# One second-weight load cut into 112, 8 and 8 rows with a small load between the last two

## The chip, the core and the metric

The kernel runs on one core of a Trainium2 chip. The metric is the device time of one execution in microseconds (us), and the median of several executions is what counts. The core has five engines with instruction streams of their own: TensorE (PE; its weight loads are listed as PEld), VectorE (DVE), ScalarE (ACT), GpSimd (POOL) and SyncE (SP). Sixteen DMA engines move data between the chip's main memory (HBM) and the core's on-chip memory of 128 partitions. An engine that issues a transfer goes on at once; a semaphore tells when the data has landed.

## The reference

Two layers follow each other. The first is attention with a sliding window, for 8 batches and 8 heads of 576 positions and 64 dimensions. Heads 0 to 3 see the last 32 positions, heads 4 to 7 every fourth of the last 128. The second is a soft mixture of experts over all 8 x 576 = 4608 tokens of 512 features:

```python
x = attn_out.transpose(0, 2, 1, 3).reshape(B * S, H * D)
logits = x @ phi                                  # 4608 x 32 slots
d = softmax of logits over the tokens             # per slot
slot_input = (d.T @ x).reshape(8, 4, 512)         # 8 experts, 4 slots each
for e in range(8):
    slot_out[e] = np.maximum(slot_input[e] @ w1[e], 0) @ w2[e]   # 512 -> 1024 -> 512
c = softmax of logits over the slots              # per token
return c @ slot_out                               # 4608 x 512, float32
```

All inputs are float32 in HBM. No expert can run before the last token's attention is done, because a slot's input sums over all tokens. w1 and w2 are 16 MB each.

## The kernel before, in words

**Work and order.** Attention runs in eight units (two batches by four heads each). For each unit POOL loads q, k and v into one of three staging buffers (`stg`), with the cast from float32 to bfloat16 done in the transfer; TensorE transposes them (L546, L551), computes scores (L589), transposes v (L614), multiplies by v (L643) and transposes the result (L671); logits and slot sums follow after every second unit (L698, L729, L746). Then come the experts: the slot sums are brought into shape (L798), the first layer (L817), a transposition (L837), the second layer (L864), row sums (L880), and at last the output product (L923, L925), its scaling on ACT and DVE (L937, L938) and the stores by SP (L946).

**The planner.** The program is a list of operations with a planned cost, a due time and dependencies. `schedule` (from L170) plays it through on a clock of its own and so fixes the order in which each engine gets its instructions; `emit` then writes waits on semaphores. POOL's and SP's operations keep the order in which they are listed. The planner has one clock, `dma_free`, for all transfers:

```python
o.dma = nbytes / 435e3 + 0.011 * nd / 16 + 0.022 * nq          # L166: nd rows, nq loads
dma_free = max(dma_free, t0 + 2.6) + o.dma                     # L200
o.end = dma_free + 1.3 + 0.004 * dma_free                      # L201: planned landing
```

Where TensorE would wait between 118 and 148 on this clock (`FILL`, L24), the planner writes fillers into its stream: matmuls whose result nobody reads (L955), planned at 0.216 each. How many is fixed when the program is written, and TensorE runs them whether or not it would have had to wait:

```python
gap = t0 - max(free[e], fill[0])                               # L243
n = min(int((gap - 0.15) / 0.216), 64)                         # L244
n = min(int((min(t0 - 0.1, fill[1]) - ts) / 0.216), 64)        # L250: ts is when TensorE is free
```

To a start after operations of another kind of tiling (`mode`) the planner adds 0.08, and 0.03 to the first such operation's cost.

**The weights.** `wload` (L437) loads w1 as eight loads of 128 rows (`w10` to `w17`, one expert each) and w2 as four pairs of experts: `p0` to `p3`, of which `p3` is cut into `p3a` and `p3b`. A pair is 128 rows of 16 chunks of 512 numbers. POOL issues them in this order, each once its place is free: w10 to w16 among the units, then w17 and p3a (in `stg` 2, when unit 5 has left it), p0 (in `stg` 0, after unit 6), p1 (in `stg` 1, after unit 7), p2 and p3b (in `TT`, when attention no longer needs it). So p3b is the last load of the queue. p0 is written in two loads of 8 chunks each (`cut`, L449), the others in one. A row of a half of p0 is 16 KB in HBM and 8192 bytes on the chip.

**Who uses them.** The second layer (L864) takes the parts in the order p3a, p0, p1, p2, p3b; the first three are 80 matmuls in one stretch, p2 is 32, p3b is 16. Behind p3b's matmuls stand the slots' scaling (`so_sb`, L891 and L895), and behind that the whole output. The places of w17, p0 and w10 to w16 are used again to stage the output.

Of the kernel before, what the change touches and what calls it, by code (L numbers as in the profile page):

```python
# [129 lines left out]
class Prog:  # L130
# [7 lines left out]
    def op(self, e, fn, r=(), w=(), a=(), alloc=(), cost=0.5, key=0.0, mode="f",  # L138
           sem=None, nbytes=0, nd=0, nq=1, ni=2, after=()):
        o = Op(e, fn, cost, key, mode)  # L140
        deps = list(after)
        for b in r:
            deps += b.ready
        for b in w:
            b.fresh()
            deps += b.prev
        for b in a:
            deps += b.prev
        seen = set()
        for d in deps:  # L150
            if d.id not in seen:
                seen.add(d.id)
                o.deps.append(d)
        for b in r:
            b.reads.append(o)
        for b in list(w) + list(a):
            b.ready.append(o)
        o.wr = [b for b in list(w) + list(a) if b.pool is not None]
        for b in list(r) + list(w) + list(a):
            if b.pool is not None and b not in o.touch:  # L160
                b.left += 1
                o.touch.append(b)
        o.alloc = list(alloc)
        o.sems = sem
        o.ni = ni + 2
        o.dma = nbytes / 435e3 + 0.011 * nd / 16 + 0.022 * nq  # L166
        self.ops.append(o)
        return o
# [147 lines left out]
def bass_dilated_sliding_attn__then__soft_moe_slots_kernel(  # L316
# [12 lines left out]
    op = P.op  # L329

    def sb(name, shape, dt=BF16):
        return A(nc.sbuf_tensor(name, shape, dt))
# [3 lines left out]
    stg = sb("stg", [128, 3, 9216])  # L336
# [22 lines left out]
    h_sb = sb("h_sb", [128, FF])  # L359
    hT = sb("hT", [128, 16, 128])  # L360
    half = sb("half", [128, 2, 32])
    so_sb = sb("so_sb", [128, DM])

    ps = A(nc.psum_tensor("ps", [128, 8, 512], F32))
# [19 lines left out]
    def pair(t):  # L384
        return ps[:, t.phys[0]:t.phys[0] + 2, :]
# [11 lines left out]
    b_stg = [Buf() for _ in range(3)]  # L397
# [30 lines left out]
    HOME = {}  # L428
    b_home = []

    def home(ap, al, name):
        b = Buf()
        b.al = al
        HOME[name] = (ap, b)
        b_home.append((ap, b))

    def wload(name):  # L437
        ap, b = HOME[name]
        b.prev = [o for al in b.al for o in al.ready + al.reads]
        sem = DmaSem(nc, f"s_{name}")  # L440
        if name[:2] == "w1":
            src = moe_w1[int(name[2:])].rearrange("(p c) f -> p c f", c=4)
            dst = ap.rearrange("p (c f) -> p c f", c=4)
        else:
            g = int(name[1])
            c = {"": slice(0, 16), "a": slice(0, 8), "b": slice(8, 16)}[name[2:]]
            src = moe_w2[2 * g:2 * g + 2].rearrange("e (p c) f -> (e p) c f", c=16)[:, c, :]
            dst = ap.rearrange("p (c f) -> p c f", f=512)
        cut = [slice(0, 8), slice(8, 16)] if name == "p0" else [slice(None)]  # L449
        op("pool", lambda g: [g.dma_start(dst[:, x], src[:, x]) for x in cut], after=b.prev, a=[b],  # L450
           cost=0.6 * len(cut), sem=sem, nbytes=512 * ap.shape[1], nd=128 * len(cut), nq=len(cut))

# [1 line left out]
        home(WD[:, e, :], [], f"w1{e}")  # L454
    home(stg[:, 2, 0:4096], [b_stg[2]], "w17")
    home(stg[:, 2, 4096:8192], [b_stg[2]], "p3a")
    home(stg[:, 0, 0:8192], [b_stg[0]], "p0")
    home(stg[:, 1, 0:8192], [b_stg[1]], "p1")
    TTf = TT[:].rearrange("p a x -> p (a x)")
    home(TTf[:, 0:8192], b_TT, "p2")  # L460
# [35 lines left out]
    for i, t in enumerate(VNt):  # L496
# [6 lines left out]
       cost=0.1, key=1)  # L503
# [31 lines left out]
    def st_T(u, j):  # L535
# [5 lines left out]
        def pe(t):  # L541
            for a in range(2):
                for kk in range(9):
# [6 lines left out]
                    for hx in range(2):  # L550
                        i_ = t.transpose(  # L551
                            bankb2(pt, a)[64 * hx:64 * hx + 64, 96 * kk:96 * kk + 96],
                            src[:, hx, c, :], ident[0:96, 0:96])
            return i_
        op("pe", pe, r=[b_id, b_stg[s]], w=[pt], alloc=[pt], cost=0.86 if ty == 0 else 0.75,
           ni=72 if ty == 0 else 36,
           mode="h" if ty == 0 else "f",
# [20 lines left out]
    def st_S(u, i):  # L578
        ty = u % 2
        sc, pt = tile(psum, 2), tile(pPT)  # L580
        U[u]["p", i] = pt

        def pe(t):
            for x in range(4):
                gi = 4 * i + x
                g, blk_ = gi // 6, gi % 6
                bpar, h01 = g // 2, g % 2
                for hx in range(2):
                    i_ = t.matmul(pair(sc)[:, hx, QB * x:QB * x + QB],  # L589
                                  win(u, 1, h01, blk_, bpar)[64 * hx:64 * hx + 64],  # L590
                                  win(u, 0, h01, blk_, bpar)[64 * hx:64 * hx + 64],
                                  start=True, stop=True)
            return i_
        k0 = due(u, 4.1 + 1.36 * i)
        op("pe", pe, r=[b_TT[u % 2]], w=[sc], alloc=[sc, pt], cost=0.28, mode="r", key=k0, ni=16)
        op("act", lambda ac: ac.activation(  # L596
            sbt(pt)[:, 0:768].rearrange("p (x n) -> p x n", x=2), pair(sc)[:, :, 0:384],
            ACTF.Exp, scale=SCALE), r=[sc], w=[pt], cost=0.71, key=k0 + 0.6)
        m0 = (4 * i) % 6

        def mk(dv):
            m = mask[ty][:, m0:m0 + 4, :].rearrange("p m x -> p (m x)")
            p_ = sbt(pt)[:, 0:768].rearrange("p (x n) -> p x n", x=2)
            return dv.tensor_tensor(p_, p_, m.unsqueeze(1).to_broadcast([128, 2, 384]), AluOp.mult)  # L604
        op("dve", mk, r=[b_mask[ty]], w=[pt], cost=0.47, key=k0 + 1.5)
# [156 lines left out]
    for u in range(NU):  # L762
        for j in range(4):
            st_T(u, j)
        if u + 3 < NU:
            for n_ in W_AFTER.get(u + 2, ()):
                wload(n_)
            load_unit(u + 3)
        else:
            if u == 5:  # L770
                for n_ in W_AFTER[7]:
                    wload(n_)
            for n_ in {5: ["w17", "p3a"], 6: ["p0"], 7: ["p1"]}[u]:
                wload(n_)
        for i in range(6):
            st_S(u, i)
        for g in range(4):
            st_V(u, g)
        for g in range(4):
            st_P(u, g)  # L780
        for bpar in range(2):
            for x in range(2):
                st_X(u, bpar, x)
        if u % 2:
            for bpar in range(2):
                st_L(u - 1 + bpar, u)
# [25 lines left out]
    for hh in range(2):  # L812
        def pe(t, hh=hh):
            for c in range(4):
                for hi in range(2):
                    for j in range(4):
                        i_ = t.matmul(pair(hp)[32 * j:32 * j + 32, hh, :], siT[:, 512 * hi + 128 * c + 32 * j:  # L817
                                                       512 * hi + 128 * c + 32 * j + 32],
                                      w1v[2 * j + hi][:, c, 512 * hh:512 * hh + 512],
                                      start=(c == 0 and hi == 0), stop=(c == 3 and hi == 1))  # L820
            return i_
        ffn1 = op("pe", pe, r=[b_siT] + w1b, a=[hp], w=[b_hp[hh]], alloc=[hp] if hh == 0 else [],
                  cost=1.8, mode="c", key=K1, ni=64)
# [32 lines left out]
    PARTS = [("p3a", 3, 0, 8), ("p0", 0, 0, 16), ("p1", 1, 0, 16), ("p2", 2, 0, 16),  # L856
             ("p3b", 3, 8, 16)]
    for k_, (name, g, c0, c1) in enumerate(PARTS):
        wv = HOME[name][0].rearrange("p (c f) -> p c f", c=c1 - c0)
        for h_ in range(2):  # L860
            def pe(t, k_=k_, g=g, c0=c0, c1=c1, h_=h_, wv=wv):
                for c in range(c0, c1):
                    j = c % 4
                    i_ = t.matmul(pair(sp_)[32 * j:32 * j + 32, h_, 0:256],  # L864
                                  hT[:, c, 24 * g:24 * g + 32],
                                  wv[:, c - c0, 256 * h_:256 * h_ + 256],
                                  start=(k_ == 0 and c < c0 + 4), stop=(k_ == 4 and c >= c1 - 4))
                return i_
            last_ = op("pe", pe, r=b_hT + [HOME[name][1]], alloc=[sp_] if k_ == h_ == 0 else [],
                       a=[sp_, b_sp[h_]], cost=0.13 * (c1 - c0) / 4, mode="c",  # L870
                       ni=2 * (c1 - c0),
                       key=K1 + 2 + 0.5 * k_ + 0.1 * h_)
            if k_ == 2:
                mid = last_
    rs = tile(psum, 1)

    def rsum(t):
# [6 lines left out]
       after=[mid])  # L884
    op("dve", lambda vv: vv.reciprocal(rtok[:], bank(rs)[:, 0:N_TOK // 128]), r=[rs], w=[b_rtok],
       cost=0.2, key=K1 + 1)
# [23 lines left out]
    for o, (t0, n) in enumerate(TILES):  # L910
# [4 lines left out]
        for j0 in range(0, n, 2):  # L915
# [4 lines left out]
            for j in range(2 if split else min(2, n - j0)):  # L920
                def pe(t, o=o, po=po, j0=j0, j=j, split=split):
                    if split:
# [4 lines left out]
                p0 = op("pe", pe, r=(b_so[j:j + 1] if split else b_so) + b_expT, a=[po],  # L927
                        w=[b_po[j]], alloc=[po] if j == 0 else [], after=[p0] if j else [],
                        cost=0.12 if split else 0.22, key=kk + 0.01 * j)
                col = rcol[o] + (0 if split else j0 + j)  # L930

                def ev(en, po=po, ost=ost, j=j, j0=j0, split=split, col=col):
# [3 lines left out]
                    if en is nc.scalar:  # L936
# [3 lines left out]
                        cost=0.35 if split else 0.6, key=kk)  # L940
# [68 lines left out]
```

## Time and profile before

| | us |
|---|---|
| median of 3 runs (lowest, highest) | 179.61 (179.53, 182.88) |
| the profiled execution | 179.53 |
| its span, first to last instruction | 177.8 |
| TensorE busy, x2621 matmuls | 135.6 |
| DVE busy | 112.9 |
| ACT busy | 96.0 |
| POOL busy | 34.4 |

The loads on POOL's queue move 30.94 MB as written on the chip (float32 becomes bfloat16 on the way); 61.93 MB are read from HBM and 9.44 MB are written to it. The time outside the span, 1.7 us, is what lies around the first and the last instruction.

How to read it: a line of a timeline gives start, duration, engine, source line, operation, tiles, and in brackets the engine's idle time before it with what ended it. A line of the windows gives for each stretch its length, the busy time of each engine with the count of instructions, the granted TensorE clock, the mean busy share of the 16 DMA engines and the GB/s that they moved. In the chain of work that ended last, each piece is followed back to what released it.

### The profile page before, as it was taken

To read this page: it belongs to the slowest core of one execution; us is meant where nothing else is said; L and a number is where in the kernel's file an instruction comes from. 1 tells how busy PE (TensorE), PEld (TensorE's weight loads), DVE (VectorE), ACT (ScalarE), POOL (GpSimd) and SP (SyncE) were. 2 spreads that over 40 slices of the span, in tenths; PEclk is the share of its full clock that TensorE was granted. 3 is DMA by queue.
4 is the path that set the end of the run, shared out by engine and by line. 5 is a ranking of instruction groups with operands and counts; after the bars stand their busy time and mean duration, and the time that the engine had idled before them with its cause. 6 is when DMAs were issued, how large, how long until landed. Compare 5 with 4: busy or idle time off the path is not lost.

```text
span 177.8 us, 5806 instructions
## 1 busy us (share of the span) xinstructions
PE 135.6 (76%) x2621; PEld 104.2 (59%) x2621; DVE 112.9 (63%) x256; ACT 96.0 (54%) x141; POOL 34.4 (19%) x69
## 2 busy tenths in 40 slices
PE   0019797779999868889859999986999999897000
PEld 0019586667887757688648888864565684332000
DVE  6850486947987986976955699899440200699200
ACT  2005888656985956696845688885401000698000
POOL 7990707005205204402000200102000000000000
PEclk9999999988999999999995799999999999999855
DMA  5999999999999999999999999999999995299995
GB/s 79 205 216 209 219 214 211 217 212 213 217 215 215 215 213 213 217 215 214 214 209 220 208 223 214 212 219 217 227 225 206 221 203 107 88 417 470 439 472 236
DMA packets 5736, 40.80 MB, mean 229 GB/s; under 512 B 1616, under 2 KB 1616, under 8 KB 2000
## 3 DMA queue, kind: packets, MB, share of 16 engines
q0 software_dynamic: 4320, 30.94, 83.9%
q1 hardware_dynamic: 1392, 9.50, 12.8%
q8 instruction: 20, 0.33, 0.7%
q14 instruction: 4, 0.03, 0.0%
HBM read 61.93 MB, written 9.44 MB: 401 GB/s over the span
## 4 chain that ended last, share of the span: by engine, by line
PE 40%; DMA 22%; DVE 16%; ACT 7%; issue 6%; POOL 2%; DVEq 0%; POOLq 0%
DMA TT<-in_moe_w_dram 17%; PE ps L551 11%; PE ps L546 6%; DVE WD L938 5%; PE ps L643 5%; DMA stg<-in_v_dram 5%; PE ps L589 5%; ACT PT L596 4%; PE ps L614 4%; PE ps L698 4%; PE ps L671 3%; DVE PT L604 3%; DVE XB L654 3%; DVE VN L619 2%; ACT TT L571 2%
## 5 line engine op out<-in xcount | busy, mean ns | idle before, releaser
L596 ACT ACTIVATE PT<-ps 128x768 bf16<-128x768 f32 x48 | 37.0, 814 | 11.7 <-PE ps L589 11.6
L571 ACT ACTIVATE TT<-ps 128x864 f32<-128x864 f32 x32 | 28.6, 897 | 21.0 <-PE ps L551 18.3
L654 DVE TENSOR_TENSOR XB<-ps,RV 96x768 bf16<-96x768 f32 x32 | 30.4, 951 | 0.9
L551 PE MATMUL ps<-ident,stg 96*64 96x96 bf16 x576 | 19.5, 238 | 14.6 <-DMA stg<-in_v_dram 12.6
L551 PEld LDWEIGHTS ps<-ident,stg 96*64 96x64 bf16 x576 | 17.4, 134 | 15.9 <-DMA stg<-in_v_dram 12.6
L619 DVE COPY VN<-ps 128x768 bf16<-128x768 bf16 x32 | 17.0, 542 | 10.4 <-PE ps L614 10.4
L589 PE MATMUL ps<-TT 64*128 64x96 bf16 x384 | 16.2, 208 | 7.3 <-issue 4.6
L643 PE MATMUL ps<-VN,PT 128*128 128x65 bf16 x384 | 18.8, 199 | 2.7 <-issue 1.0
L643 PEld LDWEIGHTS ps<-VN,PT 128*128 128x128 bf16 x384 | 15.4, 101 | 4.4 <-issue 1.2
L421 POOL DMA_DIRECT2D stg<-in_q_dram x16 | 8.5, 542 | 41.9 <-PE ps L551 26.1
L589 PEld LDWEIGHTS ps<-TT 64*128 64x128 bf16 x384 | 9.9, 95 | 11.3 <-issue 3.9
L614 PE MATMUL ps<-ident,TT 128*128 128x128 bf16 x192 | 15.7, 222 | 0.6 <-ACT PT L596 0.4
L546 PE MATMUL ps<-ident,stg 96*128 96x96 bf16 x288 | 14.7, 206 | 0.4 <-DVE XB L654 0.4
L684 ACT ACTIVATE XT<-ps 128x576 bf16<-128x576 bf16 x22 | 13.7, 652 | 2.4 <-PE ps L671 2.4
L604 DVE TENSOR_TENSOR PT<-PT,mask_d 128x768 bf16<-128x768 bf16 x24 | 13.0, 546 | 2.1 <-ACT PT L596 2.0
L546 PEld LDWEIGHTS ps<-ident,stg 96*128 96x128 bf16 x288 | 13.2, 98 | 1.3 <-DVE XB L654 0.5
L671 PE MATMUL ps<-ident,XB 96*128 96x96 bf16 x192 | 13.1, 213 | 1.1 <-DVE XB L654 1.1
L604 DVE TENSOR_TENSOR PT<-PT,mask_p 128x768 bf16<-128x768 bf16 x24 | 13.0, 552 | 1.0 <-ACT PT L596 0.4
L614 PEld LDWEIGHTS ps<-ident,TT 128*128 128x128 bf16 x192 | 11.3, 99 | 2.4 <-ACT PT L596 0.5
L671 PEld LDWEIGHTS ps<-ident,XB 96*128 96x128 bf16 x192 | 9.8, 102 | 2.8 <-DVE XB L654 1.6
L955 PE MATMUL ps<-mask_p,ident 128*128 128x512 bf16 x44 | 11.2, 379 | 0.0
L925 PE MATMUL ps<-so_sb,expT 128*128 128x512 bf16 x35 | 10.0, 395 | 0.4 <-DVE WD L938 0.2
(81 smaller groups left out, 170.8 us busy)
## 6 DMA issues: line engine op xcount, KB each, us to landing
WD<-in_moe_w_dram POOLq DMA_DIRECT2D x7, 1024.0 KB, 30.4
stg<-in_q_dram POOLq DMA_DIRECT2D x16, 288.0 KB, 19.5
stg<-in_k_dram POOLq DMA_DIRECT2D x16, 288.0 KB, 21.2
stg<-in_v_dram POOLq DMA_DIRECT2D x16, 288.0 KB, 23.2
stg<-in_moe_w_dram POOLq DMA_DIRECT2D x4, 1024.0 KB, 27.9
out_dram<-WD SPq DMA_DIRECT2D x1, 4096.0 KB, 11.9
out_dram<-WD SPq DMA_DIRECT2D x1, 2304.0 KB, 7.5
stg<-in_moe_w_dram POOLq DMA_DIRECT2D x1, 2048.0 KB, 24.4
```

The costliest lines, as they stand in the source:

```text
L546: i_ = t.transpose(bankb2(pt, a)[:, 96 * kk:96 * kk + 96], two[:, j // 2, c, :], ident[0:96, 0:96])
L551: i_ = t.transpose(bankb2(pt, a)[64 * hx:64 * hx + 64, 96 * kk:96 * kk + 96], src[:, hx, c, :], ident[0:96, 0:96])
L571: return ac.activation(d, sv, ACTF.Copy)
L589: i_ = t.matmul(pair(sc)[:, hx, QB * x:QB * x + QB], win(u, 1, h01, blk_, bpar)[64 * hx:64 * hx + 64], win(u, 0, h01, blk_, bpar)[64 * hx: ...
L596: op("act", lambda ac: ac.activation(sbt(pt)[:, 0:768].rearrange("p (x n) -> p x n", x=2), pair(sc)[:, :, 0:384], ACTF.Exp, scale=SCALE), ...
L604: return dv.tensor_tensor(p_, p_, m.unsqueeze(1).to_broadcast([128, 2, 384]), AluOp.mult)
L614: i_ = t.transpose(bankb(pv)[:, 128 * m:128 * m + 128], win(u, 2, h01, m, bpar), ident[:, :])
L619: op("dve", lambda dv: dv.tensor_copy(sbt(vn)[:, :, :, 0:64], bankb(pv)[:, 0:768].rearrange("p (m x d) -> p m x d", m=6, x=2)), r=[pv], w= ...
L643: i_ = t.matmul(pair(po)[:, bk, 65 * po_:65 * po_ + 65], sbt(pts[i])[:, o_:o_ + 128], sbt(vn)[:, m, half, 0:65], start=True, stop=True)
L654: op("dve", lambda dv: dv.tensor_tensor(sbt(xb)[:].rearrange("p m (x h d) -> p h x m d", x=2, h=2)[:, h01], pv()[:, :, :, 0:64], sbt(rv)[: ...
L671: i_ = t.transpose(bankb(px)[:, QB * m:QB * m + QB], sbt(xb)[:, m, 128 * x:128 * x + 128], ident[0:QB, 0:QB])
L684: return en.activation(d, s_, ACTF.Copy)
```

## The change

p0 gets all 9216 columns of `stg` 0 as its place. Its first 8 chunks are in columns 0 to 4095 and its last 8 in columns 4608 to 8703, so a row is two runs of 8192 bytes with a hole between them. In place of two loads of 128 rows by 8 chunks, POOL issues four loads on the same semaphore: rows 0 to 111 with all 16 chunks, rows 112 to 119, a small load of 8 rows by 2 x 32 numbers into a new scratch tile that nothing reads, and rows 120 to 127. The numbers that the planner is told change with it: cost on POOL 2.4 in place of 1.2, 288 rows in place of 256, 4 loads in place of 2; the bytes are the same. The matmuls of the second layer step over the hole (the second half of p0 begins one chunk later).

```diff
--- before.py
+++ after.py
@@ -359,6 +359,7 @@
     h_sb = sb("h_sb", [128, FF])
     hT = sb("hT", [128, 16, 128])
     half = sb("half", [128, 2, 32])
+    scr = sb("scr", [8, 2, 32])
     so_sb = sb("so_sb", [128, DM])
 
     ps = A(nc.psum_tensor("ps", [128, 8, 512], F32))
@@ -446,7 +447,18 @@
             c = {"": slice(0, 16), "a": slice(0, 8), "b": slice(8, 16)}[name[2:]]
             src = moe_w2[2 * g:2 * g + 2].rearrange("e (p c) f -> (e p) c f", c=16)[:, c, :]
             dst = ap.rearrange("p (c f) -> p c f", f=512)
-        cut = [slice(0, 8), slice(8, 16)] if name == "p0" else [slice(None)]
+        if name == "p0":
+            src = src.rearrange("p (x c) f -> p x (c f)", x=2)
+            dst = ap.rearrange("p (x y) -> p x y", x=2)[:, :, 0:4096]
+
+            def skewed(g):
+                return [g.dma_start(dst[0:112], src[0:112]), g.dma_start(dst[112:120], src[112:120]),
+                        g.dma_start(scr[0:8], src[120:128, :, 0:32]),
+                        g.dma_start(dst[120:128], src[120:128])]
+            op("pool", skewed, after=b.prev, a=[b], cost=2.4, sem=sem, nbytes=512 * 8192, nd=288,
+               nq=4)
+            return
+        cut = [slice(None)]
         op("pool", lambda g: [g.dma_start(dst[:, x], src[:, x]) for x in cut], after=b.prev, a=[b],
            cost=0.6 * len(cut), sem=sem, nbytes=512 * ap.shape[1], nd=128 * len(cut), nq=len(cut))
 
@@ -454,7 +466,7 @@
         home(WD[:, e, :], [], f"w1{e}")
     home(stg[:, 2, 0:4096], [b_stg[2]], "w17")
     home(stg[:, 2, 4096:8192], [b_stg[2]], "p3a")
-    home(stg[:, 0, 0:8192], [b_stg[0]], "p0")
+    home(stg[:, 0, :], [b_stg[0]], "p0")
     home(stg[:, 1, 0:8192], [b_stg[1]], "p1")
     TTf = TT[:].rearrange("p a x -> p (a x)")
     home(TTf[:, 0:8192], b_TT, "p2")
@@ -856,14 +868,14 @@
     PARTS = [("p3a", 3, 0, 8), ("p0", 0, 0, 16), ("p1", 1, 0, 16), ("p2", 2, 0, 16),
              ("p3b", 3, 8, 16)]
     for k_, (name, g, c0, c1) in enumerate(PARTS):
-        wv = HOME[name][0].rearrange("p (c f) -> p c f", c=c1 - c0)
+        wv = HOME[name][0].rearrange("p (c f) -> p c f", f=512)
         for h_ in range(2):
-            def pe(t, k_=k_, g=g, c0=c0, c1=c1, h_=h_, wv=wv):
+            def pe(t, k_=k_, name=name, g=g, c0=c0, c1=c1, h_=h_, wv=wv):
                 for c in range(c0, c1):
                     j = c % 4
                     i_ = t.matmul(pair(sp_)[32 * j:32 * j + 32, h_, 0:256],
                                   hT[:, c, 24 * g:24 * g + 32],
-                                  wv[:, c - c0, 256 * h_:256 * h_ + 256],
+                                  wv[:, c - c0 + (1 if name == "p0" and c > 7 else 0), 256 * h_:256 * h_ + 256],
                                   start=(k_ == 0 and c < c0 + 4), stop=(k_ == 4 and c >= c1 - 4))
                 return i_
             last_ = op("pe", pe, r=b_hT + [HOME[name][1]], alloc=[sp_] if k_ == h_ == 0 else [],
```

## The prediction

> **What bounds the kernel now.** I read the page first: the DMA row by slice, the queues, and the shares of the chain that ended last.
>
> ```profile
> PE 135.6 (76%) x2621; PEld 104.2 (59%) x2621; DVE 112.9 (63%) x256; ACT 96.0 (54%) x141; POOL 34.4 (19%) x69
> DMA  5999999999999999999999999999999995299995
> q0 software_dynamic: 4320, 30.94, 83.9%
> q8 instruction: 20, 0.33, 0.7%
> ```
>
> The 16 DMA engines work without a break from 2.7 us until about 147 us, and only then fall off (the 5 and the 2 in the row). Nearly all of it is q0, the loads that POOL issues. No compute engine is above 76%. So up to about 150 us the loads are the floor; which transfer ends it is in the chain, in order of time:
>
> ```profile
> 120.66 0.52 POOL TT L450
> 121.18 30.48 DMA TT<-in_moe_w_dram
> 151.66 0.04 issue
> 151.71 0.43 PE ps L864 x8
> 152.16 0.49 DVE so_sb L891
> ```
>
> p3b, the last load, lands at 151.66; its matmuls start 0.05 later, and 26 us of output work hang behind them. How the loads end, by windows (the last two columns are DMA share and GB/s):
>
> ```profile
> 144.00:146.00 2.00, 2.00 (x49) 1.79 (x38) 0.00 (x0) 0.00 (x0) 0.00 (x0) 1.00 1.00 209
> 146.00:148.00 2.00, 2.00 (x15) 1.05 (x15) 0.38 (x1) 0.00 (x0) 0.00 (x0) 1.00 0.86 180
> 148.00:150.00 2.00, 2.00 (x28) 0.98 (x30) 0.00 (x0) 0.00 (x0) 0.00 (x0) 1.00 0.50 106
> 150.00:152.00 2.00, 1.85 (x40) 0.90 (x32) 0.00 (x0) 0.00 (x0) 0.00 (x0) 1.00 0.11 20
> ```
>
> A share of 0.50 says that half of the engines are idle while the rest finish. The trace's packet records give start, duration, bytes and queue of each transfer, not the engine; but on one engine each record starts within 0.02 us of the end of the one before, so they link into 16 chains. I followed all 4320:
>
> - Eight chains end at 147.51 to 148.66 (mean 147.86), eight at 150.10 to 151.38 (mean 150.60): 2.74 us apart.
> - All 20 instruction fetches of q8 (16 KB each) sit in the eight late chains, three on four of them, two on the others. A fetch holds its chain up by 0.92, and the next packet is some 0.2 longer: 2.5 x 1.12 = 2.8 us. That is the whole gap.
> - A packet of p0 (8192 bytes written) starts 0.606 after the one before it; a completion record (4 bytes) puts in 0.021. The last completion is done at 151.38, and the landing is seen at 151.66, 0.28 later.
>
> Then I asked what TensorE does while the last load is awaited:
>
> ```profile
> 142.00 2.37 PE L864 MATMUL ps<-stg,hT 128*32 128x256 bf16 x80
> 144.30 2.04 PE L880 MATMUL ps<-rowm,expT 128*128 128x1 bf16 x36
> 146.20 3.40 PE L955 MATMUL ps<-mask_p,ident 128*128 128x512 bf16 x15
> 149.53 1.06 PE L864 MATMUL ps<-TT,hT 128*32 128x256 bf16 x32
> 150.52 1.04 PE L955 MATMUL ps<-mask_p,ident 128*128 128x512 bf16 x4
> 151.71 0.62 PE L864 MATMUL ps<-TT,hT 128*32 128x256 bf16 x16 [0.15 <-DMA TT<-in_moe_w_dram]
> ```
>
> It is not idle: it runs fillers (L955), written into the program by the planner. From 15 fillers to p2's matmuls is 3.33 us (149.53 - 146.20), from 3 to the 80 matmuls 0.75 (142.00 - 141.25): 0.216 each and 0.095 for the turn. Four from 150.52 are over at 150.52 + 0.86 + 0.095 = 151.48. So **p3b could start at most 0.23 us earlier, however early it lands**: 151.71 against 151.48.
>
> **The change part by part.** The sum is made against the profiled execution, 179.53 us (span 177.8, and 1.7 around it); the shown runs' median, 179.61, is 0.08 higher.
>
> *Rows moved between engines.* p0 was two loads of 128 rows, 8 rows on each engine each time: 16 packets per chain. Now the 112-row load brings 7 rows or 14 packets to each, and the 2 x 8 rows, 32 packets, go somewhere. Eight rows in whole rows fill only eight engines, and the load between them, of the same eight rows' width, is there to bring the second onto the same eight. If so, eight engines have 18 packets for p0 and eight have 14. No 8-row load is in the trace of before: the nearest rows are the 32-row loads of a unit (two rows per chain) and the 128-row ones (eight), both even. Which eight is the main unknown, since the records carry no engine numbers. If the unfetched eight: the late chains give up 2 x 0.606 = 1.21, and end at 150.17; the early ones end at 148.66 + 1.21 = 149.87. If the fetched eight: 151.38 + 1.21 = 152.59. I take the first, as the likelier of two near halves, and keep the other as an end.
>
> *Two more completions and the small load.* Two completion records are 0.04 per engine. The small load's 16 packets of 64 bytes are at least nothing and at most a p0 packet each (2 x 0.606 = 1.21 on eight engines). I take 0.02, a completion record's, as it is nearest in size: 0.04 for two. Late chains then end at 150.25, p3b lands at 150.53 (151.45 at the dear end, 151.70 if it meets an engine without relief). All but the last lie before TensorE is free.
>
> *POOL.* Four issues instead of two: the two at 99.02 take 1.05, so about 2.1. They cost nothing: behind them POOL stands 12.13 us in wait before p1 at 112.21, and p0's first packet moves only at 113.53 because the queue is full. Without this cover 1.05 us would be on p1, p2 and p3b. SP and ACT issue nothing differently.
>
> *What waits on p0.* The 80 matmuls at 142.00 wait on p3a, p0 and p1; p1's last completion is at 136.25, so even 1.3 us more is covered by 5.7. p2 is complete at 146.52, its matmuls start at 149.53 behind fillers: covered by 3. The offset by 512 columns in p0's second half changes an address, no instruction.
>
> *The planner's fillers.* This is where the gain goes. p0's planned transfer (line 166) grows by 0.011 x 32/16 + 0.022 x 2 = 0.066 us, so p1, p2 and p3b are planned 0.066 later. I use the planner's clock only to count the instructions it writes. Ahead of p2 TensorE is free there at 142.42 and p2 can start at 145.97; line 250 gives (145.97 - 0.1 - 142.42)/0.216 = 15.97, cut to the 15 that the trace shows. With 0.066 more it is 16.28: **16 fillers**. Ahead of p3b the limit is 148 (line 24): (148 - 147.04)/0.216 = 4.4 before, (148 - 147.106)/0.216 = 4.1 now: 4 still. So p2's matmuls start at 149.75 and TensorE is free for p3b at 151.48 + 0.216 = 151.70.
>
> *Sum.* p3b starts at the later of its landing + 0.05 = 150.58 and 151.70: at 151.70, against 151.71. Everything behind is the same. 179.53 - 0.01 = 179.5, or 179.6 at the median's level. The landing comes 1.1 us earlier, and TensorE's own fillers hide all of it.
>
> [...]
>
> **The rivals.**
>
> 1. *The extra rows meet the fetched engines.* Place: the eight late chains. The fullest ends at 151.38 + 1.21 + 0.04 = 152.63, p3b lands at 152.92 and its matmuls start at 152.97: +1.26, **180.8**, slower than before. It decides as soon as one chain of those ending at 150.7 to 151.4 gets two packets, as its landing then passes 151.70. For it: four such chains of 16. Against it: only that there are as many others; the records cannot decide it.
> 2. *The split does nothing:* each 8-row load is laid out evenly, one packet per engine. Then 151.38 + 0.08, landing 151.74, start 151.79: **179.6**. For it: every load in the trace is even; against: a packet here is a whole run of a row, and eight rows by sixteen engines needs a cut the 32-row loads don't show.
> 3. *An 8-row load goes to one engine:* 14 + 16 packets instead of 16 on one chain. Early chain: 147.86 + 14 x 0.606 = 156.3, landing 156.6, start 156.7, +5.0: **184.5**; a late chain, 188; both loads on one, 194. Over 2% from 6 packets too many on a late chain. Against it: no load in the trace uses fewer than 16 engines.
> 4. *No further filler* and relief as in the forecast: start at 151.48, **179.3**.
>
> **How the numbers follow.** Forecast 0.45, rival 1 0.36, rival 2 0.10, rival 3 0.05, rival 4 0.04. Leaving rival 1 out would leave out too much, so the range goes from 179.2 (rival 4 with 0.1 of spread) to 181.0 (rival 1 with 0.2). The forecast's own range is 179.2 to 179.9. Two per cent is 3.6 us, about what a measurement of this kernel can tell from no change: only rival 3 passes it, and no case gains it. Faster 0.01, same 0.94, slower 0.05.
>
> **What would show it.** Fillers: 45 in place of 44, 16 of them ahead of p2. q0's packets: 4320 + 2 x 16 + 16 = 4368. POOL at about 99: four issues in 2.1 us. p3b's landing: 29.4 us after its issue if I am right, 31.7 by rival 1, 30.5 by rival 2. The DMA share of 148 to 150 near 0.7 and of 150 to 152 near 0.03, and TensorE's wait on the DMA ahead of the last 16 matmuls gone, by the forecast; a share of 0.5 from 149 to 152 and a wait over 1 us by rival 1. If p3b lands early and the start moves with it, I am wrong on the fillers; if the stretch behind p3b differs, I am wrong that it hangs on p3b alone.

## The result and the profile after

The changed kernel took 181.97 us (median of 4 runs, 181.65 to 182.32). The kernel before took 179.53, 179.61, 182.88 and 182.94, and the ratio of the two is 1.0134, with a 95% interval of 1.0099 to 1.0169. A second series of 12 runs beside 35 of the kernel before, on one chip, gave 181.38 (179.74 to 182.84) against 179.92 (179.43 to 182.60), ratio 1.0044 (1.0002 to 1.0085). The ratios leave out runs that count as disturbed (in the first series the two slower ones of the kernel before); since both kernels spread over 3 us, and that spread is part of the answer below, the medians of all runs are given too. By the longer series the change costs 0.4% by the ratio and 0.8%, 1.46 us, by the medians; the first series has too few runs to say more. I had forecast 179.5, no change.

The page of the profiled execution (181.82 us, span 180.1), in the order in which the page before was read:

```profile
PE 138.1 (77%) x2622; PEld 106.0 (59%) x2622; DVE 112.6 (63%) x256; ACT 96.3 (53%) x141; POOL 35.8 (20%) x71
DMA  5999999999999999999999999999999994199995
q0 software_dynamic: 4416, 30.94, 83.6%
PE 54%; DVE 22%; issue 6%; DMA 5%; ACT 4%; POOL 1%; DVEq 0%; POOLq 0%
```

In the page before, the last of these lines, the shares of the chain that ended last, was:

```profile
PE 40%; DMA 22%; DVE 16%; ACT 7%; issue 6%; POOL 2%; DVEq 0%; POOLq 0%
```

One matmul more (the 16th filler). DMA has gone from the chain that ended last (22% to 5%), and TensorE has taken its place. Its timeline ahead of p3b:

```profile
144.16 2.37 PE L876 MATMUL ps<-stg,hT 128*32 128x256 bf16 x80
146.46 2.17 PE L892 MATMUL ps<-rowm,expT 128*128 128x1 bf16 x36
148.49 3.61 PE L967 MATMUL ps<-mask_p,ident 128*128 128x512 bf16 x16
152.03 1.06 PE L876 MATMUL ps<-TT,hT 128*32 128x256 bf16 x32
153.02 1.04 PE L967 MATMUL ps<-mask_p,ident 128*128 128x512 bf16 x4
153.99 0.62 PE L876 MATMUL ps<-TT,hT 128*32 128x256 bf16 x16
```

p3b's matmuls start at 153.99 without a wait on the DMA, 2.28 later than before (151.71); 181.82 - 179.53 = 2.29, so the whole loss is ahead of this point. But TensorE is late by 2.16 already at the 80 matmuls (144.16 against 142.00), before the 16th filler and before anything of p0 is used. And the load is late as well. By windows (the last three columns: granted clock, DMA share, GB/s):

```profile
124.00:126.00 2.00, 2.00 (x12) 1.14 (x10) 1.69 (x3) 0.72 (x2) 0.00 (x0) 0.50 1.35 168
126.00:128.00 2.00, 2.00 (x19) 1.21 (x18) 0.29 (x1) 0.58 (x2) 0.00 (x0) 0.67 0.75 147
...
150.00:152.00 2.00, 2.00 (x10) 0.78 (x8) 0.00 (x0) 0.00 (x0) 0.00 (x0) 1.00 0.25 53
152.00:154.00 2.00, 2.00 (x40) 1.08 (x40) 0.00 (x0) 0.00 (x0) 0.00 (x0) 1.00 0.04 8
```

Two things are new. From 124 to 128 the loads move 168 and 147 GB/s, at the handover from p0 to p1, where the kernel before moved 242 and 188:

```profile
124.00:126.00 2.00, 2.00 (x23) 1.36 (x23) 1.44 (x3) 0.75 (x4) 0.00 (x0) 1.00 1.14 242
126.00:128.00 2.00, 1.82 (x20) 1.15 (x18) 0.54 (x3) 0.54 (x1) 0.00 (x0) 1.00 0.88 188
```

And in 152 to 154 some engines still work. Linked into chains as in the prediction, the packet records say: two chains end at 147.71 and 147.95, twelve at 149.81 to 151.59, two at 152.88 and 153.08. Before, it was eight and eight, the last at 151.38. So p3b lands at about 153.36 instead of 151.66. From 123.6 to 127 many packets take up to twice as long as elsewhere (an 8192-byte one up to 1.27 us, not 0.63; a 16384-byte one up to 2.13, not 1.23); over all chains that is 19 us, 1.2 on each.

Three candidates, then: where the extra rows fall, the slowdown of all loads, and TensorE's arrival, which the granted clock of 0.50 in the first window bears on. The first theory was that the clock's stretches make the arrival late by chance and the load's layout sets a floor under it; its rival was that the longer plan (the 16th filler) pushes TensorE.

### The profile page after: what moved, and what is told of

Read it like the earlier page. It is cut to its first block, busy times and chain, and to the rows that moved or that the text cites. A ratio compares the mean times of both kernels' runs of the same rounds, so it can differ in the third digit from the quotient of the medians.

```text
span 180.1 us, 5810 instructions
## 1 busy us (share of the span) xinstructions
PE 138.1 (77%) x2622; PEld 106.0 (59%) x2622; DVE 112.6 (63%) x256; ACT 96.3 (53%) x141; POOL 35.8 (20%) x71
## 3 DMA queue, kind: packets, MB, share of 16 engines
q0 software_dynamic: 4416, 30.94, 83.6%
## 4 chain that ended last, share of the span: by engine, by line
PE 54%; DVE 22%; issue 6%; DMA 5%; ACT 4%; POOL 1%; DVEq 0%; POOLq 0%
PE ps L563 9%; PE ps L558 6%; PE ps L967 6%; PE ps L710 5%; DVE WD L950 5%; DMA stg<-in_v_dram 5%; PE ps L655 5%; DVE PT L616 4%; PE ps L626 4%; PE ps L601 4%; DVE XB L666 4%; PE ps L683 4%; DVE VN L631 4%; PE ps L741 2%; PE ps L876 2%
## 5 line engine op out<-in xcount | busy, mean ns | idle before, releaser
L563 PE MATMUL ps<-ident,stg 96*64 96x96 bf16 x576 | 18.1, 229 | 14.1 <-DMA stg<-in_v_dram 12.7
L563 PEld LDWEIGHTS ps<-ident,stg 96*64 96x64 bf16 x576 | 16.2, 127 | 15.4 <-DMA stg<-in_v_dram 12.7
L626 PE MATMUL ps<-ident,TT 128*128 128x128 bf16 x192 | 17.2, 234 | 0.5 <-ACT PT L608 0.4
L601 PEld LDWEIGHTS ps<-TT 64*128 64x128 bf16 x384 | 10.5, 99 | 9.4 <-issue 3.1
L626 PEld LDWEIGHTS ps<-ident,TT 128*128 128x128 bf16 x192 | 12.1, 104 | 2.8 <-ACT PT L608 0.5
L683 PEld LDWEIGHTS ps<-ident,XB 96*128 96x128 bf16 x192 | 10.4, 104 | 4.6 <-issue 2.5
L967 PE MATMUL ps<-mask_p,ident 128*128 128x512 bf16 x45 | 12.0, 396 | 0.0
L710 PE MATMUL ps<-XT,phi_pad 128*128 128x192 bf16 (+1 forms) x64 | 10.6, 316 | 0.2 <-DVE expX L722 0.2
```

What stands on the lines that cost most here:

```text
L563: i_ = t.transpose(bankb2(pt, a)[64 * hx:64 * hx + 64, 96 * kk:96 * kk + 96], src[:, hx, c, :], ident[0:96, 0:96])
L601: i_ = t.matmul(pair(sc)[:, hx, QB * x:QB * x + QB], win(u, 1, h01, blk_, bpar)[64 * hx:64 * hx + 64], win(u, 0, h01, blk_, bpar)[64 * hx: ...
L626: i_ = t.transpose(bankb(pv)[:, 128 * m:128 * m + 128], win(u, 2, h01, m, bpar), ident[:, :])
L683: i_ = t.transpose(bankb(px)[:, QB * m:QB * m + QB], sbt(xb)[:, m, 128 * x:128 * x + 128], ident[0:QB, 0:QB])
L967: i_ = te.matmul(bank(t)[:, 0:512], ident[:, :], mask[0][:].rearrange("p m x -> p (m x)")[:, 0:512], start=True, stop=True)
```

## The experiments

All 18 runs with a profile at a glance; "start" is the start of p3b's matmuls, the later of landing and arrival, "extra" the time that packets took beyond their usual, summed over the chains around 121 to 129:

| run | last chain ends | extra | 80 matmuls start | start | profiled run | runs: median (range) |
|---|---|---|---|---|---|---|
| before | 151.38 | 0 | 142.00 | 151.71 | 179.53 | |
| after | 153.08 | 19 | 144.16 | 153.99 | 181.82 | 181.97 (181.65-182.32) |
| e1 after again | 153.50 | 21 | 139.42 | 153.87 | 182.84 | 181.38 (179.74-182.84) |
| e2 before again | 151.71 | 0 | 141.11 | 152.01 | 179.84 | 180.36 (179.75-181.76) |
| e3 split only | 152.68 | 22 | 142.94 | 153.05 | 180.88 | 181.56 (180.58-183.13) |
| e4 told only | 151.26 | 0 | 143.67 | 153.59 | 181.40 | 180.61 (179.68-183.46) |
| e5 no small load | 152.71 | 14 | 144.56 | 154.25 | 182.06 | 180.94 (180.25-182.47) |
| e6 two on | 152.66 | 9 | 141.80 | 153.02 | 181.14 | 181.16 (180.05-183.17) |
| e7 fourteen on | 152.76 | 3 | 142.75 | 153.07 | 180.90 | 181.49 (180.84-182.95) |
| e8 spread rows | 151.14 | 0 | 141.09 | 151.51 | 179.38 | 180.95 (179.38-181.83) |
| e9 late fillers off | 151.55 | 0 | 142.45 | 151.87 | 180.57 | 180.60 (180.08-180.90) |
| e10 spread, late off | 152.45 | 0 | 143.82 | 152.82 | 181.62 | 181.50 (180.45-181.64, one 206.0) |
| e11 probe | 153.00 | 20 | 143.77 | 153.74 | 181.58 | |
| e12 no fillers | 151.55 | 0 | 146.21 | 151.86 | 180.62 | 180.61 (179.65-182.91) |
| e13 one small load | 151.60 | 0 | 144.19 | 153.70 | 181.53 | |
| e14 main in four | 153.53 | 25 | 142.19 | 153.90 | 181.74 | |
| e15 fillers to 146 | 151.33 | 0 | 141.92 | 151.66 | 179.45 | 179.71 (179.33-181.19) |
| e16 112 and 16 rows | 152.38 | 10 | 141.47 | 152.68 | 180.53 | 180.86 (180.51-182.47) |
| e17 eight narrow | 153.39 | 36 | 140.25 | 153.74 | 181.54 | |
| e18 eight spread | 151.60 | 0 | 140.54 | 151.95 | 180.30 | |

The kernel before, timed beside them, had medians of 179.92 (e1 to e4), 180.10 (e5 to e8), 179.77 (e9 to e12) and 180.03 (e13 to e16).

**Each half of the change alone.** e1 and e2 are the two kernels unaltered.

> The changed kernel once more, unaltered. Its profile had p3b landing about 153.4 and TensorE's own stream arriving at p3b's matmuls at 153.99, 2.3 us later than before, with four half-clock stretches of the granted clock (17 us) ahead of the last matmul where the kernel before had two (10 us). Rows theory (the load's layout sets a floor): p3b lands near 153.4 again, no run below 181.2, and the slowdown of all loads near 124 is there again. Clock theory (half-clock stretches fall where they fall): the runs spread, some near 181.2 and some above 182, and the stretches lie elsewhere in this profile; the landing near 153.4 is not explained by it.

> The kernel before once more, unaltered, as a control. Clock theory: its runs fall in two heaps, near 179.6 and near 182.9, as the four known ones do, and where it is slow TensorE reaches p3b late while p3b still lands near 151.7. Rows theory says nothing of the upper heap, but p3b must land near 151.7 in the profile whatever the time is. If all runs are near 179.6, the upper heap was the chip's and not the clock's.

e3 keeps the four loads and tells the planner the old numbers; e4 does the reverse:

```diff
-            op("pool", skewed, after=b.prev, a=[b], cost=2.4, sem=sem, nbytes=512 * 8192, nd=288,
-               nq=4)
+            op("pool", skewed, after=b.prev, a=[b], cost=1.2, sem=sem, nbytes=512 * 8192, nd=256,
+               nq=2)
```

> The four loads of p0 as in the change, but the planner is told the old numbers, so TensorE gets 15 fillers ahead of p2 and every engine's order is that of before. Rows theory: p3b lands near 153.4, floor 181.2, the same as the change. Planner theory (the 16th filler, or the longer plan, is what pushes TensorE): back to 179.6. Clock theory: 179.6 to 182.9 by chance, but not below the landing's floor if there is one.

```diff
+        told = (2.4, 288, 4) if name == "p0" else (0.6, 128, 1)
         op("pool", lambda g: [g.dma_start(dst[:, x], src[:, x]) for x in cut], after=b.prev, a=[b],
-           cost=0.6 * len(cut), sem=sem, nbytes=512 * ap.shape[1], nd=128 * len(cut), nq=len(cut))
+           cost=told[0], sem=sem, nbytes=512 * ap.shape[1], nd=told[1], nq=told[2])
```

> The two loads of p0 as before, but the planner is told the change's numbers, so TensorE gets the 16th filler ahead of p2. Rows theory: as the kernel before, p3b lands near 151.7, 179.6 in its lower heap (plus 0.0 to 0.2 for the filler). Planner theory: 181.8 as the change. Clock theory: two heaps as before.

The timelines of TensorE at p2 and p3b, first e3, then e4:

```profile
150.47 1.06 PE L876 MATMUL ps<-TT,hT 128*32 128x256 bf16 x32
...
153.05 0.62 PE L876 MATMUL ps<-TT,hT 128*32 128x256 bf16 x16 [0.55 <-DMA TT<-in_moe_w_dram]
```

```profile
151.63 1.06 PE L865 MATMUL ps<-TT,hT 128*32 128x256 bf16 x32
...
153.59 0.62 PE L865 MATMUL ps<-TT,hT 128*32 128x256 bf16 x16
```

In e3 TensorE came early and stood 0.55 in wait for the load: the split alone puts the landing at 152.96, and the runs at a median of +1.64 over the kernel before. In e4 the load was complete at 151.26, as before, and TensorE came 1.9 late by itself: 181.40 with nothing of the split in it. But e4's median is 0.69 above that of the kernel before, with a ratio of 1.001 (0.9971 to 1.0049): the planner theory's 181.8 is out, and what the 16th filler's 0.2 is worth can't be told from nothing. The clock theory's two heaps fell too: of the 35 runs beside e1 to e4, 21 lie between 179.4 and 180.1, and the rest trail off to 182.6. And the floor of 181.2 fell: e1 had a run at 179.74 and two more below 180.5. What stands is that start plus 27.8 is the time wherever TensorE's clock stays up (27.79 to 27.87 in fourteen of the twenty rows above), and that two things set the start, the landing and TensorE's arrival. By this sum the run at 179.74 started p3b near 151.9, so the changed kernel's landing too moves from execution to execution; no profile caught it that early, and why is open.

**Where the extra rows go.** e5 drops the small load, e6 and e7 add another ahead of the first 8-row load (2 and 14 rows; `scr` is made wider):

```diff
-                        g.dma_start(scr[0:8], src[120:128, :, 0:32]),
```

> The change without the small load between the two 8-row loads. If the loads take eight engines each, one after the other around the sixteen, every engine now gets 16 packets for p0, as before, and the chains end in two heaps 2.7 us apart again, as before the change. Layout theory of the slowdown near 124 (eight engines crowd into eight partitions): the slowdown stays, about 1 us on every chain, and p3b lands near 152.7. Small-load theory (the 64-byte load and its many 4-byte records slow all): no slowdown, p3b lands near 151.8. If the 8-row loads always start at the same engine, the ends stay as with the change, two chains far behind, p3b near 153.4.

```diff
-                return [g.dma_start(dst[0:112], src[0:112]), g.dma_start(dst[112:120], src[112:120]),
-                        g.dma_start(scr[0:8], src[120:128, :, 0:32]),
+                return [g.dma_start(dst[0:112], src[0:112]), g.dma_start(scr[0:2, 2:4], src[0:2, :, 0:32]),
+                        g.dma_start(dst[112:120], src[112:120]),
+                        g.dma_start(scr[0:8, 0:2], src[120:128, :, 0:32]),
```

> The change with one more small load, of 2 rows, ahead of the first 8-row load. The changed kernel's chains show that six of the eight engines with extra rows are unfetched and two are fetched. Cursor theory: the 2-row load moves the start by two, so the extra rows meet either no fetched engine (all chains end within about 2 us, p3b lands near 151.4 with the slowdown, 150.5 without) or four (four chains far behind, p3b near 153.5). Rival, no cursor: two far-behind chains as in the change, p3b near 153.4.

> The same with 14 rows in the added small load in place of 2. Cursor theory: the start moves by fourteen, that is back by two: what the 2-row load does not hit, this one does, so one of the two kernels has no far-behind chain and the other has four. Rival, no cursor: as the change in both.

I call a chain fetched when instruction fetches sit in it. Without the small load (e5), six of the unfetched chains had the first 8-row load and the other two the second, eight chains each. In the change (and in e1, e3 and e8), with the small load between them, the second 8-row load was on the same eight as the first, as I had taken it. But six of these eight are unfetched and two are fetched: these two end last, and the two unfetched ones that got no row end 4 to 5 us ahead of them. Two places on, four chains were far behind (151.28 to 152.66), as the cursor theory had it for one of the two kernels; but fourteen on did not clear the others: one chain was at 152.76, and two fetched ones still had extra rows. So, if a short load moves the place on by its rows, which no run shows, the fetched engines are not eight in a row, and my hope to meet the unfetched ones by one shift fell. A probe with sixteen one-row loads, meant to number the places, did not do so:

```diff
+        PR = [17, 19, 23, 29, 31, 37, 41, 43, 47, 53, 59, 61, 67, 71, 73, 79] if name == "p0" else []
+        op("pool", lambda g: [g.dma_start(dst[:, x], src[:, x]) for x in cut]
+           + [g.dma_start(stg[0:1, 0, 8192 + sum(PR[:i]):8192 + sum(PR[:i + 1])], moe_w2[0, 0:1, 0:n])
+              for i, n in enumerate(PR)], after=b.prev, a=[b],
```

> The kernel before with sixteen one-row loads behind p0, each of a different odd size (17 to 79 numbers), into unused columns. It measures which chain takes which place in the order in which short loads go round. Cursor theory: each of the sixteen loads falls on another chain, and the unfetched eight include six of the first eight places. Rival: the loads all fall on one chain.

All sixteen ran on one chain, 0.028 to 0.036 apart. The 20 us of extra time in this run are of another kind than the change's: p0's packets are as fast as before, and sixteen packets alone, the first of p1 on each chain, right behind some thirty 4-byte records, take 2.15 to 2.68 us instead of 1.23.

**What slows all loads.** e8 keeps the shares and changes which rows they are (and cuts the other 112 rows into four loads, which e14 below does alone):

```diff
-                return [g.dma_start(dst[0:112], src[0:112]), g.dma_start(dst[112:120], src[112:120]),
-                        g.dma_start(scr[0:8], src[120:128, :, 0:32]),
-                        g.dma_start(dst[120:128], src[120:128])]
+                r = [slice(1, 128, 4), slice(2, 128, 4), slice(3, 128, 4), slice(0, 64, 4),
+                     slice(64, 96, 4), slice(96, 128, 4)]
+                res = [g.dma_start(dst[x], src[x]) for x in r[:5]]
+                res.append(g.dma_start(scr[0:8], src[120:128, :, 0:32]))
+                return res + [g.dma_start(dst[r[5]], src[r[5]])]
```

> The same shares per engine as the change, but the rows of the 8-row loads lie four partitions apart (64 to 92 and 96 to 124), and the other 112 rows come in three loads of 32 and one of 16. Layout theory: the slowdown of all loads near 124 is gone, so p3b lands about 1 us earlier than with the change, near 152.5 with the two far-behind chains. Small-load theory: the slowdown stays, p3b near 153.4 or later.

```profile
148.83 1.06 PE L878 MATMUL ps<-TT,hT 128*32 128x256 bf16 x32
149.82 1.04 PE L969 MATMUL ps<-mask_p,ident 128*128 128x512 bf16 x3
151.51 0.62 PE L878 MATMUL ps<-TT,hT 128*32 128x256 bf16 x16 [0.66 <-DMA TT<-in_moe_w_dram]
```

(The 1.04 us of fillers are the length of four, as before; the trace keeps three of their records.) The extra time was gone, and p3b landed 1.9 earlier than in the change, with two fetched chains last again (151.13 and 151.14, two fetches each). Not all of the 1.9 is the rows: e10 below has the same loads and no extra time either, and its two last chains ended at 151.95 and 152.45, a landing near 152.73. In time the gain is not shown: e8's ratio to the kernel before, 1.0025 (0.9987 to 1.0063), and the change's, 1.0044, overlap. e13, e14 and e16 went on to part the rest; e13 adds one small load behind the old halves of p0, e14 cuts the 112 rows into 32, 32, 32 and 16, e16 leaves all short loads out:

```diff
-                return [g.dma_start(dst[0:112], src[0:112]), g.dma_start(dst[112:120], src[112:120]),
-                        g.dma_start(scr[0:8], src[120:128, :, 0:32]),
-                        g.dma_start(dst[120:128], src[120:128])]
+                return [g.dma_start(dst[0:112], src[0:112]), g.dma_start(dst[112:128], src[112:128])]
```

> The kernel before with one small load (8 rows of 2 x 32 numbers, into unused columns) behind p0's two loads. If any load on fewer than sixteen engines slows the others, the slowdown near 124 is there (some 1 us per chain, p3b near 152.7). If it takes the narrow rows or the 112-row load, no slowdown, p3b near 151.8.

> The change with the 112 rows in four loads (32, 32, 32 and 16 rows), the 8-row loads and the small load as in the change. Narrow-rows theory: the slowdown stays, p3b near 153.4. 112-row theory: it goes, p3b near 152.0 with the two fetched chains behind.

> p0 as one load of 112 rows and one of 16, no 8-row load and no small load, the planner told as in the change. Every engine gets 16 packets as before. 112-row theory: the slowdown is there, p3b near 152.7. Short-load theory: none, p3b near 151.7, and the runs lie as those of the kernel before with 16 fillers (179.7 to 182).

The small load costs nothing (e13: 0). The 112-row load is not needed (e14: 25). And 16 adjacent rows over sixteen engines bring half of it (e16: 10), which neither theory had: it goes with the adjacency, not with the short load. The last pair differs only in which rows make up a load: half of p0 in eight loads of 8 rows, adjacent in e17, four partitions apart in e18 (the lines in place of the change's four loads):

```diff
+                return [g.dma_start(dst[0:64], src[0:64])] + [
+                    g.dma_start(dst[x:x + 8], src[x:x + 8]) for x in range(64, 128, 8)]
```

```diff
+                return [g.dma_start(dst[0:64], src[0:64])] + [
+                    g.dma_start(dst[x:x + 29:4], src[x:x + 29:4])
+                    for x in (64, 65, 66, 67, 96, 97, 98, 99)]
```

> p0 as one load of 64 rows and eight loads of 8 adjacent rows, which go round the engines evenly (16 packets each), planner told as in the change. Narrow-rows theory: four times as many packets in narrow loads as in the change, so the packets' extra time, 19 us over all chains there, is 50 us or more, and p3b lands after 154. Rival (the handover to p1 is slow by itself, whatever the layout): near 20 us again.

> The same with the rows of each 8-row load four partitions apart. Narrow-rows theory: no extra time, p3b lands near 151.9. Rival: near 20 us of extra time as in the other.

Windows of e17, then of e18:

```profile
122.00:124.00 2.00, 2.00 (x23) 1.27 (x22) 1.44 (x4) 0.75 (x2) 0.00 (x0) 1.00 1.24 148
124.00:126.00 2.00, 1.81 (x18) 0.98 (x16) 0.80 (x3) 0.80 (x3) 0.00 (x0) 1.00 1.08 143
```

```profile
122.00:124.00 2.00, 1.99 (x19) 1.12 (x19) 1.53 (x3) 0.75 (x3) 0.00 (x0) 1.00 1.15 230
124.00:126.00 2.00, 1.82 (x19) 1.01 (x16) 0.99 (x3) 1.08 (x3) 0.00 (x0) 1.00 1.08 225
```

148 and 143 GB/s against 230 and 225, and p3b's start 1.79 apart (153.74, 151.95). The extra time was 36, not the 50 I had expected from counting packets, but the pair, one profile each, shows what mattered here: with short loads of adjacent rows all loads were slow, and with the same loads of rows four apart they were not. What about adjacent rows does it is not shown. In every one of these edits the rows lie side by side, or apart, in HBM as well as on the chip's partitions, and no run moves the one without the other. Why e7 had only 3 us, and e6 9, with the same narrow rows also stays open.

**What makes TensorE late.** e9 ends the filler window at 140, so that the 15 and the 4 fillers are not written; e10 does so with e8's rows; e12 writes no fillers at all (`FILL = (0, 0)`):

```diff
-FILL = (118, 148)
+FILL = (118, 140)
```

> The kernel before with the planner's filler window ended at 140 in place of 148: the 15 and the 4 fillers ahead of p2 and p3b are not written. Theory: the start of p3b's matmuls is the later of the landing and TensorE's own arrival, and it is the arrival that makes the upper heap. Without 19 fillers (4.1 us) the arrival is always earlier than the landing, so p3b starts 0.05 after it lands, near 151.7 to 152.0, and the runs close up near 179.5 to 180.0, none above 180.5. Rival: the fillers keep TensorE's clock up, and without them the runs are slower than before.

> The spread rows (8-row loads four partitions apart) together with the filler window ended at 140. Theory: the start is the landing, and the landing is set by the two fetched engines with extra rows, near 151.4 when these have two fetches, up to 152.6 with three: 179.3 to 180.5. Rival: as in the run without late fillers.

> The kernel before with no fillers at all (44 fewer matmuls). Theory: as with the late ones off, 179.5 to 180.0, since the landing of p3b is then the limit in every run. Rival (the fillers keep the clock up): slower than before by 0.5 or more, with more half-clock stretches or slower matmuls ahead of p3b.

e9 in windows and in TensorE's timeline:

```profile
148.00:152.00 4.00, 0.17 (x8) 0.13 (x8) 0.00 (x0) 0.00 (x0) 0.00 (x0) 0.54 0.31 66
```

```profile
146.98 1.06 PE L864 MATMUL ps<-TT,hT 128*32 128x256 bf16 x32 [0.19 <-DMA TT<-in_moe_w_dram]
151.87 1.04 PE L864 MATMUL ps<-TT,hT 128*32 128x256 bf16 x16 [3.83 <-DMA TT<-in_moe_w_dram]
```

Both sides were half right. The spread went, from 2.7 us in the kernel before timed beside it to 0.8 (180.08 to 180.90), which says that it had been the arrival. But the median rose by 0.83, and the profile shows where: TensorE idled 3.83 us, its granted clock was 0.54 over 148 to 152 and 0.61 over 152 to 156, p3b's matmuls took 1.04 instead of 0.62, and the time behind the start was 28.70, not 27.8. e10 and e12 paid the same (28.80 and 28.76), e12 with a wait of only 0.24 right ahead of p3b. e10's runs, 181.50, so lie above the 179.3 to 180.5 that I had expected. e15 takes away only the 4 fillers ahead of p3b:

```diff
-FILL = (118, 148)
+FILL = (118, 146)
```

> The kernel before with the filler window ended at 146: the 4 fillers ahead of p3b are not written, the 15 ahead of p2 stay. TensorE arrives 0.96 us earlier. Theory: fast runs stay at 179.5 to 179.7 (the landing), slow runs come down by up to 0.96, so the median falls by some 0.2 and the highest run by near 1. Rival: a wait of about 1.2 us for p3b already costs the clock, as 3.8 us did (+0.9 on every run).

```profile
149.45 1.06 PE L864 MATMUL ps<-TT,hT 128*32 128x256 bf16 x32
151.66 0.62 PE L864 MATMUL ps<-TT,hT 128*32 128x256 bf16 x16 [1.14 <-DMA TT<-in_moe_w_dram]
```

With this wait of 1.14 p3b's matmuls still took 0.62, and behind the start lay 27.79. Between 1.14 and 3.83 the profiles go both ways: waits of 1.94 (e14) and 2.23 (e17) left 27.8 behind the start, but 1.46 (e6) came with 28.12 and 1.64 (e18) with 28.35, the granted clock at 0.51 from 156 to 158 in the one and 0.50 from 154 to 156 in the other. The median of e15 was 179.71 against 180.03, the highest run 181.19 against 183.18. The ratio of 0.9978 (0.9943 to 1.0013) includes 1, so it is not shown to be faster.

The stretches of half clock go with the arrival, mostly; this compares profiles, and no run changed the clock alone. Up to p3b they lasted 3.41 and 6.83 us in the profile of before, and 6.83 and three times 3.41 in that of after, and they lie elsewhere in each execution. Where a profile had 10 to 14 us of them ahead of 130 (and the same fillers up to there), the 80 matmuls started between 139.42 and 142.94; with 17 to 21 us, between 141.92 and 144.56. The profiles of after, e10, e11 and e13 had one from about 123 to 127, close ahead of the 80 matmuls: 143.77 to 144.19. e14's, from 122.0 to 125.4, came with only 142.19. One kernel (before and e2) had stretches at 38 and 93 in one execution, and at 33, 43, 70 and 94 in the other.

## Why the prediction was wrong

- **What bounds the kernel: right, but only for the execution that I read.** "p3b could start at most 0.23 us earlier" holds there. I took TensorE's arrival, 151.48, for a property of the program. Over the executions it moves by some 5 us (the 80 matmuls start between 139.42 and 144.56 where the fillers ahead of them are the same), with e4 and e13 at 153.6 and 153.7 although p3b had landed by 151.9. The three runs shown reached 182.88, and I left that unexplained.
- **Two heaps of chains, set apart by the fetches: right.** In every run here without moved rows the chains end in two heaps, and with the change's rows the two fetched chains that got some end last.
- **"Rows moved between engines": the step that failed.** I took the unfetched eight, and kept the fetched eight as the other end. It was six of the one and two of the other, so that the last two chains ended at 152.88 and 153.08, and p3b landed at 153.36, where I had 150.53. That meets rival 1's condition as I had put it ("as soon as one chain of those ending at 150.7 to 151.4 gets two packets"), near its landing: 152.92 forecast, 152.96 to 153.78 measured in the three profiles of this split. That it came so near is in part luck, because 1.2 of the measured lateness is the next term, which rival 1 did not have; with the rows spread the landings were 151.42 (e8) and 152.73 (e10). I had weighed two neat halves and no mixture, so rival 1 stood at 0.36 where a start at a random place makes it much the likelier.
- **A term that was not in the sum: the narrow rows.** I priced a packet at 0.606 wherever it goes. In the narrow loads and beside them it took up to 1.27, and the larger ones of p1 up to 2.13; that is 1.2 on every chain, and with spread rows it is gone. Whether the change would still cost anything without it can't be told from e8's ratio of 1.0025 (0.9987 to 1.0063).
- **The planner's fillers: right.** 45 in all, 16 ahead of p2, 4 ahead of p3b. That this hides an earlier landing was not put to the test, since the landing came later.
- **POOL, completions: right in price, wrong in count.** Four issues took 2.38 at 97.44 (1.27, 0.56 and 0.55), ahead of p1 at 112.92. q0 had 4416 packets, not 4368: an engine that had no part in an 8-row load still wrote three records of 4 bytes. The dear end that I gave for the small load's landing, 151.45, does not come out of its terms: 150.17 + 0.04 + 1.21 + 0.28 is 151.70. Nothing hung on it, as the small load's packets took 0.026 to 0.035 each.
- **"Everything behind is the same": right** at 27.8, until TensorE's clock drops around a wait; with e9's 3.83 us that is 0.9 more, with e18's 1.64 us 0.5.

So two losses were each taken as zero: the landing's 1.3 to 2.1 us (152.96 to 153.78 against 151.66) and the arrival's 0 to 2.5. In the profiled execution it was the arrival that came last, 153.99; had TensorE come in time, the landing would have cost 1.7.

## What to carry to other kernels

When two paths meet within 0.2 us, one profile does not say where either stands: look at how far the runs spread, and ask which of the paths moves from execution to execution, before forecasting to tenths. Moving rows between DMA engines also changes which rows make up a load: try the rows of a short load apart (four partitions here), because short loads of whole adjacent rows cost packet time in every run that had them (3 to 36 us, summed over the chains, against 0 with the rows four apart). Fillers that kept the clock up (without them the granted clock fell to 0.54 in e9) also made TensorE late when it was held up before (by 1.9 us in e4). Here a wait of about 1 us was free and one of 4 us cost 0.9; in between, the profiles went both ways.

## What the runs showed of the hardware

- In the kernel before all 20 instruction fetches of 16 KB went through the same eight of sixteen DMA engines, 0.92 us each, and the loads there ended 2.7 us behind the others.
- In e5 the first 8-row load ran on eight engines and the second on the other eight; in e11 sixteen one-row loads ran on a single one. On the engines that had no part in them, each of the change's three loads of 8 rows left three 4-byte records.
- With eight loads of 8 adjacent rows all loads together moved 148 GB/s where the same loads with rows four apart moved 230 (e17, e18).
- With a wait of 3.83 us TensorE's granted clock was 0.54 over 148 to 152 and 0.61 over 152 to 156 (e9); with 1.14 us p3b's matmuls ran at full speed (0.62 us, e15).
- Behind some thirty 4-byte records in a row the next 16384-byte packet took 2.15 to 2.68 us instead of 1.23, on every chain (e11).
